# Six buffers for v, six PSUM banks for the first tile's scores, and three loads moved to ACT's queue

## The chip, the cores and the metric

The kernel runs on one core of one Trainium2 chip. The metric is the time on the device in microseconds (us); lower is better. All of the work is done in one launch.

## The reference

Attention with two small matrices that mix the heads, before and after the softmax, followed by two feed-forward layers. B = 4 batches, H = 12 heads, S = 448 positions, D = 64; the layers have 1792 tokens, a model width of 768 and inner widths of 1536 and 2048.

```python
scores = scale * np.matmul(q, k.transpose(0, 1, 3, 2))
scores = np.einsum('bhij,hg->bgij', scores, w_pre)
attn = np.exp(scores - np.max(scores, axis=-1, keepdims=True))
attn = attn / (np.sum(attn, axis=-1, keepdims=True) + 1e-09)
attn = np.einsum('bhij,hg->bgij', attn, w_post)
x = np.matmul(attn, v)                      # then laid out as (1792, 768)
x = (1 / (1 + np.exp(-(x @ w_gate))) * (x @ w_val)) @ w_out
h = np.maximum(x @ w_in, 0.0)
out = (h * h) @ w_out2
```

## The kernel before

The program is written in an order by hand: each engine, and each queue of transfers, runs its instructions in the order in which the Python code emits them, and waits only where an operand or a buffer isn't ready. The engines are TensorE (PE), VectorE (DVE), ScalarE (ACT), GpSimd (POOL) and SyncE (SP). SP issues nearly all transfers, in one queue; ACT can issue some from its own.

**Attention** (`attention`, first some 490 us). Each batch's 448 rows are cut into four row tiles of 120, 120, 100 and 108 rows (`tiles`), and each tile into groups of 10 rows (`groups`), 180 in all. Two tiles make a chunk (`chunks`), eight in all. The main loop (L384) goes over steps s, one group each:

- `scores(n, p)` (L188): for tile n and the pair p of heads, two matmuls (L201; four instructions in the trace) into two PSUM banks of the pool `ps_q`, which has two; ACT copies one bank out (L213), DVE the other (L211), into an `e` buffer (three buffers; in tile 0 the pairs from 3 on use the free buffers of another pool); then transfers `g<-e` (L223) spread the rows over partitions. In tile 0 the rows are in two blocks: the first block's transfers go out at once, some from ACT's queue, the second block's are kept in `second` and go out after all six pairs (L382).
- `premix(s)` (L229): the first mixing matrix `wp` times the spread scores (L237), for two groups, into banks of the pool `ps_m`, which has four.
- `maximum`, `exponent`, `normal` (L245 to L271): the softmax, and the second mixing matrix scaled by the rows' sums (`wn`, on POOL at L266; in the last 14 groups on ACT at L270).
- `postmix(s)` (L275): the second mixing (L282), copied by DVE into `ap` (L294).
- `values(c, h)` (L304): for a chunk c and two heads, 16 matmuls of `ap` and the v tile `vraw` (L311), copied by ACT to `xo` (L326) and stored to `xs` (L327).

Before the loop, the queries and keys of the first tile are loaded in three parts (L373), `masks()` (L127) clears buffers on POOL, loads `w_pre` and `w_post` into `wr` by three small transfers on SP's queue (L133, L137) and makes masks; then come the six `scores(0, p)`, the next tile's queries, and `mixers()` (L155), which makes `wp` and `wq` out of masks and `wr` on DVE.

**The v tiles.** `v_load` (L299) loads one tile of two heads; a chunk uses six of them. The pool `a_v` has four buffers. The first four loads are emitted at steps 4 to 7. After `values` for heads h and h + 1, a buffer is free: if the chunk has another tile to come beyond the four, its load is emitted right then (with the next `flush`), otherwise the buffer is counted in `freed[1]` and filled at one of the next odd steps:

```python
if f is values and (x[1] + 2) % HV == 0:
    if x[1] + 2 + 4 * HV <= H:
        pending.append((load_next, v_load, v_order))
    else:
        freed[1] += 1
```

**The feed-forward layers** (`mlp`) come after. Their work is put in by a planner, `Feed`: tasks have costs, due times (`need`) and buffers out of stocks, and `feed.step` emits those that fit beside the attention's steps; all matmuls of this part are emitted by `feed.finish()` after the attention. Beside the attention it already converts weights (`raw`, `y`, `gv` in the rows) and, from the time on when the last scores are emitted, loads the first inputs `t<-xs` and splits each into two parts (L885: ACT L888, then DVE L891). A split's output takes a buffer of the stock `slots`: five exist from the start (L716), eleven more once the last `postmix` is emitted (`after_mixes`, L723).

Of the kernel before, what the change touches and what calls it, by code (L numbers as in the profile page):

```python
# [9 lines left out]
F32 = mybir.dt.float32  # L10
# [9 lines left out]
P = 128  # L20
JP = 112
GI = 10
HV = 2
# [4 lines left out]
HP = P // 2  # L28
MW, PW, VW, SW, STEP = 0.40, 0.85, 1.66, 0.92, 2.2
KB = 10  # L30
UT = 6


# [34 lines left out]
def attention(tc, feed, q, k, v, w_pre, w_post, xs, B, H, S, D):  # L68
# [10 lines left out]
    nc = tc.nc  # L79
# [22 lines left out]
    with ExitStack() as ctx, ExitStack() as mid, ExitStack() as left:  # L102
        kw = dict(side="right")
        one = ctx.enter_context(tc.tile_pool(name="a_one", bufs=1, **kw))
        pv4 = ctx.enter_context(tc.tile_pool(name="a_v", bufs=4, **kw))
        po = ctx.enter_context(tc.tile_pool(name="a_o", bufs=4, **kw))
        pp = ctx.enter_context(tc.tile_pool(name="a_p", bufs=1, **kw))
        pa = mid.enter_context(tc.tile_pool(name="a_a", bufs=NA, **kw))
# [2 lines left out]
        ps_q = mid.enter_context(tc.tile_pool(name="ps_q", bufs=2, space=PSUM, side="left"))  # L111
# [15 lines left out]
        def masks():  # L127
            nc.gpsimd.memset(wr, 0.0)
            nc.gpsimd.memset(mask, 0.0)
            nc.gpsimd.memset(wp, 0.0)  # L130
            for g in g_of:
                nc.gpsimd.memset(g[:G0], 0.0)
            nc.sync.dma_start(  # L133
                out=wr[G0 : G0 + GI * H, 0, :], in_=w_pre.unsqueeze(0).to_broadcast([GI, H, H])
            )
            for u in range(2):
                nc.sync.dma_start(  # L137
                    out=wr[u * HP : u * HP + KH, 1, :],
                    in_=w_post.unsqueeze(0).to_broadcast([HB, H, H]),
                )  # L140
            for u, m in ((0, first), (0, mask[:HP, :HB]), (1, mask[HP:, HB:])):
                nc.gpsimd.memset(m, 1.0)
                lead = G0 if m is first else 0
                for base, mult in ((-lead, 1), (H - 1 + lead, -1)):
                    nc.gpsimd.affine_select(
                        out=m,
                        in_=m,
                        compare_op=ALU.is_ge,
                        fill=0.0,
                        base=base,  # L150
                        pattern=[[-mult * H, HB], [0, H]],
                        channel_multiplier=mult,
                    )
# [34 lines left out]
        def scores(n, p):  # L188
# [3 lines left out]
            if p == 0:  # L192
                g_t[n] = g_of[n % 2]
            kt = k_t.pop((b, p)) if i0 + rows == S else k_t[b, p]
            ps = [
                ps_q.tile([P, S], F32, tag="q", name="ps_s")
                for _ in range(2)
            ]
            for o in range(2):
                r = slice(o * D, (o + 1) * D)  # L200
                nc.tensor.matmul(  # L201
# [176 lines left out]
        for p in range(NP):  # L378
            scores(0, p)
# [4 lines left out]
        for s in range(NG + 30):  # L384
# [2 lines left out]
            flush()  # L387
            if s < NG:
                maximum(s)
            if s in (4, 5, 6, 7):  # L390
                load_next(v_load, v_order)
            if s >= 8 and s % 4 == 0 and freed[0]:
                load_next(k_load, k_order)
# [14 lines left out]
            while bpos < len(back) and (left_over > 0.5 or s >= NG or late or back[bpos][0] is values and not made):  # L408
# [15 lines left out]
                f(*x)  # L424
                made = made or f is values
                if f is values and (x[1] + 2) % HV == 0:
                    if x[1] + 2 + 4 * HV <= H:
                        pending.append((load_next, v_load, v_order))
                    else:
                        freed[1] += 1  # L430
# [262 lines left out]
def mlp(ctx, tc, xs, wg, wv, wo, wi2, wo2, out):  # L693
# [6 lines left out]
    feed = Feed(tc)  # L700
# [9 lines left out]
    def pool(name, bufs, **kw):  # L710
        return ctx.enter_context(tc.tile_pool(name=name, bufs=bufs, reuse_waits="tile", **kw))
# [1 line left out]
    raws, ys, w32s, ws, slots, brief, xts, cs, gs, banks = (Stock() for _ in range(10))  # L713
    feed.stock(raws, pool("m_r", 2, side="left"), 2)
    feed.stock(ys, pool("m_y", 2, side="left"), 2)
    feed.stock(slots, pool("m_s0", 5, side="left"), 5)  # L716
    dram = pool("m_dram", 1, space=DRAM)

    def after_scores():
# [4 lines left out]
    def after_mixes():  # L724
        feed.stock(w32s, pool("m_w31", 1, side="left"), 1)
        feed.stock(ws, pool("m_w1", 1, side="left"), 1)
        feed.stock(slots, pool("m_s1", 11, side="left"), 11)
        feed.stock(banks, pool("m_ps0", 6, space=PSUM, side="left"), 6)

    def after_all():  # L730
# [473 lines left out]
```

## Time and profile before

| | |
|---|---|
| median of three timed runs | 1369.6 us (1364.2 to 1371.24) |
| the profiled execution | 1377.83 us |
| its span, first to last instruction | 1376.1 us |
| PE busy | 1322.3 us, 96% of the span |
| PE weight load busy | 1067.6 us, 78% |
| DVE busy | 1086.5 us, 79% |
| ACT busy | 764.7 us, 56% |
| POOL busy | 329.3 us, 24% |

All times below are us from the start of the span. A row of the timeline gives the start and the length of one instruction or of several alike in a row (x4 is four), and in brackets how long the engine had been idle just before, and what ended that. "SPq" and "ACTq" are the queues of SP and ACT: their rows are the issuing of transfers, not the transfers themselves. The "granted clock" is TensorE's clock as a share of 2.4 GHz. The DMA share is the mean busy share of the core's 16 transfer engines.

### The profile page before, as it was taken

What the parts mean: (1) busy time and instruction counts of PE and PEld (TensorE: products, weight loads), DVE (VectorE), ACT (ScalarE), POOL (GpSimd) and SP (SyncE); (2) the same over time, 40 slices, a digit from 0 to 9 for tenths busy, and PEclk for the clock granted to TensorE, in tenths of its full rate; (3) what the DMA queues carried; (4) which work ended last, traced back from release to release, by engine and by line L of the source; (5) the groups of instructions that cost most, each with busy time, mean ns of one, the idle gap of its engine ahead of it and who ended that gap; (6) DMA issues with size and microseconds to landing.
All of it is one profiled execution on the core that took longest, in us unless ns stands there. A gap on an engine that the chain in (4) does not pass through costs nothing.

```text
span 1376.1 us, 22485 instructions
## 1 busy us (share of the span) xinstructions
PE 1322.3 (96%) x7604; PEld 1067.6 (78%) x7604; DVE 1086.5 (79%) x1953; ACT 764.7 (56%) x1434; POOL 329.3 (24%) x353
## 2 busy tenths in 40 slices
PE   6879999999999899999999999999999999999998
PEld 2445555564655689999999999999988999999998
DVE  2767786786878878789998788999998986566864
ACT  2544544454455665667666666676655565434553
POOL 3243343343344204340022433003430000000000
PEclk9999999999999999999999999999999999999999
DMA  4768758877676747987478888549885455333343
GB/s 153 232 175 233 235 187 238 235 231 228 206 235 202 266 135 252 318 274 232 119 255 298 309 296 276 164 137 323 281 288 155 119 159 171 104 105 105 112 124 106
DMA packets 146478, 284.61 MB, mean 207 GB/s; under 512 B 17276, under 2 KB 91708, under 8 KB 146364
## 3 DMA queue, kind: packets, MB, share of 16 engines
q1 hardware_dynamic: 145984, 282.61, 65.2%
q8 instruction: 60, 0.98, 0.3%
q10 hardware_dynamic: 380, 0.57, 0.1%
q14 instruction: 54, 0.44, 0.1%
HBM read 180.25 MB, written 63.31 MB: 177 GB/s over the span
## 4 chain that ended last, share of the span: by engine, by line
PE 87%; DVE 5%; DMA 5%; ACT 1%; issue 1%; POOL 0%; SPq 0%; ACTq 0%; DVEq 0%; POOLq 0%
PE ps L903 63%; PE ps_p L282 8%; PE ps_s L201 6%; PE ps_v L311 5%; PE ps_m L237 5%; DMA g<-e 2%; DMA vraw<-in_v 2%; DVE ap L294 2%; DVE nm L248 1%; DVE e L211 1%; DVE y L782 1%; DMA k<-in_k 0%; DVE y L779 0%; ACT e L213 0%; DMA gv<-y 0%
## 5 line engine op out<-in xcount | busy, mean ns | idle before, releaser
L903 PE MATMUL ps<-s,w 128*128 128x448 f32 x4284 | 876.9, 367 | 3.8 <-DVE w L891 3.8
L903 PEld LDWEIGHTS ps<-s,w 128*128 128x128 f32 x4284 | 805.6, 188 | 74.8 <-DVE w L891 4.1
L891 DVE TENSOR_TENSOR w<-w,w 128x768 fp32r<-128x768 f32 x238 | 248.5, 1046 | 95.4 <-ACT w L888 93.8
L888 ACT CAST w<-w 128x768 fp32r<-128x768 f32 x238 | 199.0, 836 | 167.4 <-PE ps L903 147.0
L793 POOL TENSOR_TENSOR y<-y,raw 128x384 int32<-128x384 int32 x136 | 166.9, 1245 | 425.3 <-DVE y L782 127.2
L282 PEld LDWEIGHTS ps_p<-wn,a 128*112 128x112 f32 x1440 | 156.8, 176 | 94.1 <-POOL wn L266 40.2
L282 PE MATMUL ps_p<-wn,a 128*112 128x120 f32 x1440 | 182.0, 274 | 18.7 <-DVE ap L294 8.3
L266 POOL TENSOR_SCALAR wn<-wq,sm 128x120 f32<-128x120 f32 x166 | 113.2, 682 | 274.3 <-DVE sm L263 214.7
L248 DVE TENSOR_REDUCE nm<-ps_m 128x1 f32<-128x448 f32 x180 | 111.0, 617 | 60.0 <-PE ps_m L237 59.9
L255 ACT ACTIVATE a<-ps_m,nm 128x448 f32<-128x448 f32 x180 | 114.4, 636 | 60.3 <-DVE sm L260 52.0
L888 ACT CAST s<-g 128x448 fp32r<-128x448 f32 x196 | 109.9, 566 | 40.5 <-PE ps L903 35.2
L891 DVE TENSOR_TENSOR s<-g,s 128x448 fp32r<-128x448 f32 x196 | 122.0, 633 | 4.6 <-ACT s L888 0.6
L294 DVE COPY ap<-ps_p 112x480 f32<-112x480 f32 x180 | 114.1, 648 | 10.2 <-PE ps_p L282 8.3
L213 ACT COPY e<-ps_s 120x448 f32<-120x448 f32 (+1 forms) x96 | 51.1, 532 | 120.4 <-PE ps_s L201 93.7
L201 PE MATMUL ps_s<-k,q 64*120 64x448 f32 (+1 forms) x384 | 105.1, 615 | 13.1 <-ACT e L213 7.7
L211 DVE COPY e<-ps_s 120x448 f32<-120x448 f32 (+1 forms) x96 | 60.0, 625 | 47.0 <-PE ps_s L201 30.3
L311 PE MATMUL ps_v<-ap,vraw 112*64 112x240 f32 (+1 forms) x768 | 85.7, 369 | 10.8 <-DMA vraw<-in_v 9.4
L237 PE MATMUL ps_m<-g,wp 64*64 64x448 f32 x720 | 92.2, 572 | 3.9 <-DMA g<-e 3.8
L311 PEld LDWEIGHTS ps_v<-ap,vraw 112*64 112x64 f32 x768 | 54.5, 140 | 52.7 <-ACT xo L326 14.4
L201 PEld LDWEIGHTS ps_s<-k,q 64*120 64x120 f32 (+1 forms) x384 | 29.8, 182 | 58.3 <-ACT a L255 17.6
L928 DVE TENSOR_TENSOR c<-ps,c 128x448 f32<-128x448 f32 x104 | 63.9, 619 | 10.1 <-PE ps L903 9.4
L773 ACT ACTIVATE raw<-raw 128x768 f32<-128x768 f32 x68 | 62.0, 912 | 11.9 <-DMA raw<-in_wo 5.2
(44 smaller groups left out, 830.5 us busy)
## 6 DMA issues: line engine op xcount, KB each, us to landing
w<-wo SPq DMA_DIRECT2D x98, 384.0 KB
w<-gv SPq DMA_DIRECT2D x84, 384.0 KB
g<-e SPq DMA_DIRECT2D x132, 210.0 KB
raw<-in_wo SPq DMA_DIRECT2D x56, 384.0 KB
w<-wi SPq DMA_DIRECT2D x56, 384.0 KB
wo<-y SPq DMA_DIRECT2D x42, 384.0 KB
gv<-y SPq DMA_DIRECT2D x36, 384.0 KB
raw<-in_wi SPq DMA_DIRECT2D x32, 384.0 KB
```

What stands on the lines that cost most here:

```text
L201: nc.tensor.matmul(ps[o][:isz], lhsT=q_t[n][r, p, :isz], rhs=kt[r], start=True, stop=True)
L237: nc.tensor.matmul(ps[u * HP : (u + 1) * HP], lhsT=wp[r], rhs=g_t[n][r, 2 * t + u], start=True, stop=True,)
L248: nc.vector.tensor_reduce(out=nm, in_=ps, op=ALU.max, axis=AX.X, negate=True)
L255: nc.scalar.activation(a, ps, AF.Exp, bias=nm, accum_out=sm)
L266: nc.gpsimd.tensor_scalar(out=wn, in0=wq, scalar1=sm, scalar2=None, op0=ALU.mult)
L282: nc.tensor.matmul(ps[:JP, jt], lhsT=a[:, jt * JP : (jt + 1) * JP], rhs=wn.rearrange("p g i -> p (g i)"), start=True, stop=True,)
L294: nc.vector.tensor_copy(ap[c][:, :, :, g0 - i0 : g0 - i0 + rows], ps[:JP, :, :, :rows])
L311: nc.tensor.matmul(ps[o * D : (o + 1) * D, :w], lhsT=vraw[c, (h + o) // HV][:, (h + o) % HV, jt, :], rhs=ap[c][:, jt, h + o, :w], start=jt ...
L793: e.tensor_tensor(out=y3, in0=y3, in1=word(0)[:, i].bitcast(I32), op=ALU.add)
L888: e.copy(dst.tile[:, 0], src.tile)
L891: e.tensor_tensor(out=dst.tile[:, 1], in0=src.tile, in1=dst.tile[:, 0].bitcast(F32), op=ALU.subtract)
L903: e.matmul(bank.tile, lhsT=a[k], rhs=x[l], start=start and n == 0, stop=stop and n == 2, skip_group_check=not fresh,)
```

## The change

- The pool `a_v` gets six buffers (`VB`). The first six v loads are emitted at steps 4 to 9, and each buffer that comes free is then filled at one of the next odd steps (the condition `x[1] + 2 + 6 * 2 <= 12` never holds).
- In tile 0 the pairs 1, 2, 4 and 5 take their two banks from `ps_m`, the pairs 0 and 3 from `ps_q`.
- The three loads of `w_pre` and `w_post` are issued from ACT's queue.
- Of the sixteen `slots`, three in place of five exist from the start, and thirteen in place of eleven come with `after_mixes`.

```diff
+VB = 6
-        pv4 = ctx.enter_context(tc.tile_pool(name="a_v", bufs=4, **kw))
+        pv4 = ctx.enter_context(tc.tile_pool(name="a_v", bufs=VB, **kw))
...
-            nc.sync.dma_start(
+            nc.scalar.dma_start(
                 out=wr[G0 : G0 + GI * H, 0, :], in_=w_pre.unsqueeze(0).to_broadcast([GI, H, H])
             )
             for u in range(2):
-                nc.sync.dma_start(
+                nc.scalar.dma_start(
                     out=wr[u * HP : u * HP + KH, 1, :],
...
-            ps = [
-                ps_q.tile([P, S], F32, tag="q", name="ps_s")
-                for _ in range(2)
-            ]
+            at, tag = (ps_m, "m") if n == 0 and p % 3 else (ps_q, "q")
+            ps = [at.tile([P, S], F32, tag=tag, name="ps_s") for _ in range(2)]
...
-            if s in (4, 5, 6, 7):
+            if 4 <= s < 4 + VB:
                 load_next(v_load, v_order)
...
-                    if x[1] + 2 + 4 * HV <= H:
+                    if x[1] + 2 + VB * HV <= H:
...
-    feed.stock(slots, pool("m_s0", 5, side="left"), 5)
+    feed.stock(slots, pool("m_s0", 3, side="left"), 3)
...
-        feed.stock(slots, pool("m_s1", 11, side="left"), 11)
+        feed.stock(slots, pool("m_s1", 13, side="left"), 13)
```

## Rows read from the trace of the kernel before

**Rows 1.** Busy time by stage: PE, PEld, DVE, ACT, POOL; clock, DMA share.

```profile
0.00:490.00 490.00, 443.43 (x3310) 260.60 (x3312) 360.22 (x909) 233.97 (x575) 182.28 (x242) 0.99 0.71 216
490.00:1376.00 886.00, 878.88 (x4298) 807.03 (x4292) 726.26 (x1044) 530.78 (x859) 147.04 (x111) 1.00 0.63 202
```

**Rows 2.** Timeline of the head: start, length, engine, line, output<-input, count, [idle].

```profile
4.02 1.85 PE L201 MATMUL ps_s<-k,q 64*120 64x448 f32 x4 [4.02 <-DMA k<-in_k]
...
5.10 1.00 SPq L133 DMA_DIRECT2D wr<-in_w_pre  x1
5.87 0.53 ACT L213 COPY e<-ps_s 120x448 f32<-120x448 f32 x1 [3.80 <-PE ps_s L201]
5.91 0.62 DVE L211 COPY e<-ps_s 120x448 f32<-120x448 f32 x1 [5.91 <-PE ps_s L201]
6.15 1.54 SPq L137 DMA_DIRECT2D wr<-in_w_post  x2
...
6.59 1.85 PE L201 MATMUL ps_s<-k,q 64*120 64x448 f32 x4 [0.72 <-DVE e L211]
7.81 12.07 SPq L223 DMA_DIRECT2D g<-e  x8
...
11.89 0.59 POOL L145 TENSOR_SCALAR_AFFINE_SELECT mask<-mask 64x60 f32<-64x60 f32 x2
...
16.69 2.08 PE L201 MATMUL ps_s<-k,q 64*120 64x448 f32 x4 [0.48 <-ACT e L213]
16.90 0.78 ACTq L223 DMA_DIRECT2D g<-e  x1
18.57 0.53 ACT L213 COPY e<-ps_s 120x448 f32<-120x448 f32 x1 [1.93 <-PE ps_s L201]
...
20.46 9.45 SPq L383 DMA_DIRECT2D g<-e  x10
22.59 1.77 PE L237 MATMUL ps_m<-g,wp 64*64 64x448 f32 x8 [3.82 <-DMA g<-e]
```

**Rows 3.** Waits: engine, line <- releaser: us in total, times, longest.

```profile
PE ps_v L311 <- DMA vraw<-in_v: 9.4, 3, 4.9
```

**Rows 4.** Timeline of PE, first chunk's values.

```profile
97.94 1.84 PE L311 MATMUL ps_v<-ap,vraw 112*64 112x240 f32 x16
104.66 3.45 PE L311 MATMUL ps_v<-ap,vraw 112*64 112x240 f32 x16 [4.87 <-DMA vraw<-in_v]
108.04 0.98 PE L237 MATMUL ps_m<-g,wp 64*64 64x448 f32 x8
```

**Rows 5.** Busy time in slices of 2 us, same stretch.

```profile
101.00:103.00 2.00, 0.00 (x0) 0.00 (x0) 0.08 (x1) 0.00 (x0) 0.53 (x1) 1.00 1.00 345
...
105.00:107.00 2.00, 2.00 (x12) 1.35 (x10) 0.00 (x0) 0.00 (x0) 0.00 (x0) 0.50 0.80 267
```

**Rows 6.** Timeline of PE, third and fifth chunk's values.

```profile
220.25 3.18 PE L311 MATMUL ps_v<-ap,vraw 112*64 112x240 f32 x16 [2.31 <-DMA vraw<-in_v]
...
335.81 2.69 PE L311 MATMUL ps_v<-ap,vraw 112*64 112x240 f32 x16 [2.19 <-DMA vraw<-in_v]
338.44 1.76 PE L237 MATMUL ps_m<-g,wp 64*64 64x448 f32 x8
```

**Rows 7.** Busy time, 20 us in the seventh chunk's values.

```profile
430.00:450.00 20.00, 18.91 (x151) 9.86 (x152) 12.31 (x33) 10.19 (x27) 6.28 (x10) 1.00 0.77 240
```

**Rows 8.** Chain of work that ended last: start, us, what.

```profile
83.46 10.06 DMA g<-e
...
97.33 7.19 DMA vraw<-in_v
```

**Rows 9.** Timeline of SP's queue around steps 8 and 9.

```profile
45.20 2.06 SPq L769 DMA_DIRECT2D raw<-in_wg  x3
51.65 1.68 SPq L223 DMA_DIRECT2D g<-e  x2
```

**Rows 10.** Timeline of PE at the end of the mixing steps.

```profile
473.44 1.07 PE L282 MATMUL ps_p<-wn,a 128*112 128x120 f32 x8 [0.77 <-ACT wn L270]
```

## The prediction

> **What bounds the kernel now.** First the stages [rows 1]: in the first 490 us (attention) TensorE (PE) is busy 443.43 us, so it sits idle for 46.6; in the 886 us after them (the two feed-forward layers) it is idle for 7.1. TensorE is the bound in both, and only the first has idle time worth taking. The change touches the first, and the hand-over. Then the timeline of the head [rows 2] and the waits of TensorE in the 490 us. The largest wait for a transfer that repeats is the one of the values step (L311) for `vraw`: 9.4 us in 3 places [rows 3], at 104.66, 220.25 and 335.81 [rows 4, 6].
>
> The profiled execution took 1377.83 us with a span of 1376.1, so 1.7 us lie around the span; the median of the three timed runs is 1369.6. The sum is a saving, worked out within the span, and taken off the median. Within 0.5% (6.85 us) a measurement of this kernel could hardly tell from no change.
>
> **First tile's scores, six banks.** Six pairs of heads each run L201, and each needs two PSUM banks that ACT (0.53) and DVE (0.62) copy out [rows 2]. With two banks, pair p+1 can't start before both copies of pair p are done: TensorE takes 1.85, then idles 0.72 or a little less. From the first pair at 4.02 to the sixth at 16.69 that is 12.67 for five, 2.53 each. With six banks pair p+1 runs while pair p is copied, and a bank comes back two pairs later. Banks of the mixing step are borrowed; its first use of them is at 22.59, after all copies.
> Two prices. At 1.85 a pair, five periods save 5 x (2.53 - 1.85) = 3.4 us. But 1.85 is a low clock: the same eight instructions of the mixing step take 1.77 at 22.59 and 0.98 at 108.04 [rows 2, 4]. After the stall that ends at 104.66 TensorE worked without a break at a granted clock of 0.50 (1.2 GHz), and by 108.04 had 2.4 GHz again [rows 4, 5]. (In the head the column of the granted clock reads 1.00 although the durations are doubled; there I go by the durations.) In the head before, TensorE breaks off after each pair and its sixth pair still takes 2.08; after, it runs unbroken from 4.02, so I expect the faster level for the last three pairs or so, at 1.85 x 0.98/1.77 = 1.02 each. ACT is next late then: on pairs 3 to 5 it copies (0.53) and issues a `g<-e` transfer (0.78) [rows 2], 1.31 per pair. Pairs 0 and 1 end at 5.87 and 7.72, pair 2 about 9.3, pair 3 about 10.3; then copy, issue, copy, issue, copy on ACT bring the sixth copy's end to 10.3 + 0.53 x 3 + 0.78 x 2, about 13.5, where it now is 18.57 + 0.53 = 19.10 [rows 2]: 5.6 us saved.
> What follows is tied to the sixth copy: SP's ten second-block transfers, 9.45 us without a pause, directly behind the next q load, and the mixing step at 22.59 that waits for `g<-e` [rows 2]. Both move with it. The masks on POOL end at 11.89 + 0.59, in time. I take 5.0, nearer to the faster level; ends 3.4 and 6.0.
>
> **Mixing weights on ACT's queue.** SP loses three issues, 1.00 + 1.54 = 2.54 us [rows 2], and its first `g<-e` could go out at the end of the first copy, 6.40, in place of 7.81. SP isn't what ends the head (it waits for the copies), so I add nothing. ACT gains three issues; it is idle for 3.80 before its first copy at 5.87 [rows 2], which holds 2.54 or, at a slower first issue, some 3.3. What waits behind them is that copy, then TensorE. Without this cover the cost is 2.54. The loads also run beside the first q and k loads now, not behind them; nearest row: the k load on which the first scores wait (4.02 of idle, [rows 2]). Bounds: 0.5 gained to 1 lost; I take 0, since by their shapes the three loads move some 11 KB and one k load 224.
>
> **Six buffers for v.** Each chunk of rows uses six v tiles, of two heads each. With four buffers the fifth and sixth can be loaded only when the first and second have been used, and this in a stretch in which the transfer engines are full (share 1.00 at 101 to 103, [rows 5]). In the first chunk the fifth tile's load is issued at 97.33 and takes 7.19 [rows 8]; TensorE, done with the fourth at 97.94 + 1.84 = 99.78, waits for it until 104.66 [rows 4]. With six buffers all six of a chunk are loaded while the chunk before is finished, one per two steps, tens of us ahead. So all three waits should go: 4.87 + 2.31 + 2.19 = 9.37 us [rows 4, 6].
> Each also brings a low clock behind it: sixteen matmuls take 3.45, 3.18 and 2.69 in place of 1.84, and the mixing step at 338.44 takes 1.76 in place of 0.98 [rows 4 to 6]: 1.61 + 1.34 + 0.85 + 0.78 = 4.58. Together 13.95 us at most. A chunk of the same size that met no such wait shows that the other engines can keep pace: 18.91 of 20 us busy at 430 to 450 [rows 7].
> Not all of it stays. In these stretches the `g<-e` transfers are slow as well; one is in the chain for 10.06 us [rows 8], and scores, whose output buffers (three) wait for them, are next late. I take two thirds, 9.5; ends 4.7 (a third) and 14.0.
> The Trainium skill (DMA: Bandwidth & Descriptors, Issuing engines are not separate DMA queues) has a rule that speaks against more: transfers of all queues share the same 16 engines, and another queue saves only the time of issuing. By that, a v tile that lands earlier takes its time from another transfer, and the result would be that of the second rival below, 1362.6 and not 1355.1. The trace agrees that the engines are full at the first stall (1.00, [rows 5]); it shows a share of 0.77 at the chunk without a wait [rows 7], so that there is room elsewhere.
> The two loads that are added at the start, at steps 8 and 9, cost SP 2 x 0.5 us; SP has nothing from 47.26 to 51.65 [rows 9], so nothing is added (1 us if that cover is gone). Later ones move by a step or two; the same number is issued, behind the same stores.
>
> **Three early slots for five.** Two of five split inputs of the feed-forward layer (ACT about 0.55 and DVE about 0.6 each) can no longer be made before the last mixing step. There TensorE waits for ACT (0.77 at 473.44, [rows 10]): a gain of up to 0.8 per split, 1.6. They are made during the last values, when ACT is lightly used; if not, 2 x 0.55 is lost at the hand-over. I take 0; ends 1.6 gained, 1.1 lost.
>
> **Sum**: 5.0 + 0 + 9.5 + 0 = 14.5 us, of the profiled 1377.8 to about 1363.3, and of the median to **1355.1**. All ends at their best: 6.0 + 0.5 + 14.0 + 1.6 = 22, 1347.5. All at their worst: 3.4 - 1 + 4.7 - 1 - 1.1 = 5, 1364.6.
>
> **Rivals.** *All of it* stays: nothing else is late, 5.6 + 13.95, about 1350. For: the undisturbed chunk [rows 7]. Against: [rows 8].
> *The transfers are the next wait.* The v stalls go, but the scores' `g<-e` transfers, which used the pause to land, are late in their place: 4 from the head and 3 from the stalls, 7 us, 1362.6 (1359 to 1367). For: share 1.00 and landings of 7.19 and 10.06 us [rows 5, 8]. Against: SP is held by `vraw` less, and bytes don't grow.
> *The change doesn't do what it says* in the head: the low clock stays, and ACT's three new issues hold the first copy up by their 2.54, so 3.4 - 2.5 = 0.9; of the stalls a fifth comes back, 2.8: 3.7 in all, 1365.9. Against it is the unbroken work after 104.66 that did bring the clock up [rows 4, 5].
> *Slower*: the extra v traffic at each chunk makes `g<-e` late in all tiles. From the point on where such a transfer lands later than the three buffers last, scores stop in every tile. Priced like the second stall's idle time, 2.31 [rows 6], in the 14 tiles after the head: 32 us lost against 14.5 gained, 1387. For: one landing of 10.06 did hold up ACT [rows 8]. Against: this needs it in every tile, and bytes are unchanged.
>
> **How the numbers follow.** Forecast 0.52 (1350 to 1360 by itself), all of it 0.12, transfers next 0.24, head fails 0.06, slower 0.06. Faster by over 0.5% means under 1362.8: 0.52 + 0.12 + half of 0.24 = 0.76. Within: 0.12 + 0.06 = 0.18. Slower 0.06. The range of 8 in 10 leaves out the slower case, the failed head, and the outer parts of the first two rivals (some 0.03 and 0.05): 1347 to 1365.
>
> **What would show it.** Right: six L201 calls at the start without the 0.7 us pauses, the last ones near 1 us; the first L237 at about 17 and not 22.59; no L311 row with `vraw` as its releaser; the last values at about 475 and not 490. Wrong: L237 at 19 or later (the clock or ACT); new waits of the scores for `g<-e` at 90 to 105; a TensorE pause between the last values and the first L903. The forecast fails most likely at the size of the v term.

## The result, and the profile after

In twenty timed runs of each kernel the changed kernel took 1359.55 us (median, 1352.29 to 1373.32) and the kernel before 1372.41 (1364.2 to 1389.07): a ratio of 0.9894, with a 95% interval of 0.9871 to 0.9916. On the 1369.6 us from which the prediction started, that is a saving of 14.5 us (11.5 to 17.7). The two medians by themselves are 12.9 us apart; the ratio, which leaves out runs over 1.5% above the fastest of their kernel, is what the text goes by. A second comparison of the same two kernels (below) gave 0.9923, a saving of 10.5 us (5.2 to 15.9). Predicted were 14.5 and a time of 1355.1, in a range of 1347 to 1365. The sum came out as forecast, to the tenth by luck; the terms behind it did not all do so, and that is what the rest is about.

The profiled execution took 1360.46 us with a span of 1358.7; before it was 1377.83 and 1376.1. Busy time by stage in the kernel after, with the columns of [rows 1] (the last values step ended at 490.36 before and ends at 479.65 now; the same first stretch is shown so that the lines can be compared):

```profile
0.00:490.00 490.00, 449.15 (x3362) 269.39 (x3363) 367.95 (x922) 240.66 (x590) 180.50 (x242) 0.98 0.73 219
490.00:1358.00 868.00, 862.91 (x4243) 796.16 (x4241) 723.15 (x1032) 520.80 (x845) 150.43 (x111) 1.00 0.63 204
```

Of the 17.4 us between the two spans, 10.7 lie in attention (490.36 - 479.65) and 6.7 behind it, where the prediction expected nothing. The waits of TensorE in the first 490 us of the kernel after (line <- releaser: us in total, times, longest):

```profile
PE ps_p L281 <- DVE ap L293: 9.3, 14, 2.8
PE ps_m L236 <- DMA q<-in_q: 7.1, 1, 7.1
PE ps_p L281 <- POOL wn L265: 6.3, 7, 1.8
PE ps_s L200 <- ACT e L212: 5.6, 7, 2.0
...
PE ps_m L236 <- DMA gv<-y: 2.2, 1, 2.2
```

The row of [rows 3], 9.4 us of the values step waiting for `vraw`, is gone: no transfer is a releaser of L310 (L311 before) any more. New are the wait of 7.1 of the first mixing step, 3.8 before, and one of 2.2 for a transfer in the stretch where the first `vraw` wait had been.

**The head after** (start, length, engine, line, operation, count, [idle <- releaser]), to be read against [rows 2]:

```profile
0.94 1.41 ACTq L134 DMA_DIRECT2D wr<-in_w_pre  x1
...
2.38 1.55 ACTq L138 DMA_DIRECT2D wr<-in_w_post  x2
...
3.96 1.28 ACT L212 ACT_TABLE_LOAD   x1 [3.96 <-issue]
3.97 7.24 PE L200 MATMUL ps_s<-k,q 64*120 64x448 f32 x24 [3.97 <-DMA k<-in_k]
4.73 0.33 SPq L184 DMA_DIRECT2D q<-in_q  x1
5.10 2.38 SPq L176 DMA_DIRECT2D k<-in_k  x2
5.82 0.53 ACT L212 COPY e<-ps_s 120x448 f32<-120x448 f32 x1 [0.58 <-PE ps_s L200]
...
7.59 7.28 SPq L222 DMA_DIRECT2D g<-e  x8
...
12.19 0.53 ACT L212 COPY e<-ps_s 120x448 f32<-120x448 f32 x1 [0.37 <-DVE wp L160]
...
18.33 1.77 PE L236 MATMUL ps_m<-g,wp 64*64 64x448 f32 x8 [7.12 <-DMA q<-in_q]
...
24.46 1.74 PE L236 MATMUL ps_m<-g,wp 64*64 64x448 f32 x8
```

All six pairs of scores are now one unbroken row of 24 matmuls, 7.24 us long. The sixth copy on ACT ends at 12.19 + 0.53 = 12.72, 6.4 earlier than the 19.10 before. The mixing step comes only 4.26 earlier (22.59 to 18.33): TensorE waits 7.12 us for it. SP has issued the first block's eight `g<-e` by 7.59 + 7.28 = 14.87, and 3.5 us later the step starts. The row names the next tile's q load, which this step doesn't read and which was issued directly behind the eight; that the step waits for the `g<-e` to land is concluded from what it reads, and from the same row in eight of the ten profiles with six banks, the change's second one among them, which names `g<-e`.

**The first chunk's values after**, against [rows 4]:

```profile
95.70 3.46 PE L310 MATMUL ps_v<-ap,vraw 112*64 112x240 f32 x32
...
100.00 1.84 PE L310 MATMUL ps_v<-ap,vraw 112*64 112x240 f32 x16
...
105.96 0.61 PE L236 MATMUL ps_m<-g,wp 64*64 64x448 f32 x4 [2.17 <-DMA gv<-y]
```

The fifth tile's matmuls stand directly behind the fourth's (32 in one row), at the full clock, where before there were 4.87 us of idle and 3.45 us at half of it. But just behind them TensorE stops again, for 2.17 us.

### The profile page after: what moved, and what is told of

Same layout as the page of the kernel before. It is cut to its first block, busy times and chain, and to the rows that moved or that the text cites. A ratio compares the mean times of both kernels' runs of the same rounds, so it can differ in the third digit from the quotient of the medians.

```text
span 1358.7 us, 22455 instructions
## 1 busy us (share of the span) xinstructions
PE 1312.1 (97%) x7604; PEld 1065.5 (78%) x7604; DVE 1091.1 (80%) x1953; ACT 761.5 (56%) x1434; POOL 330.9 (24%) x353
## 4 chain that ended last, share of the span: by engine, by line
PE 88%; DVE 5%; DMA 5%; issue 1%; ACT 1%; POOL 0%; SPq 0%; DVEq 0%; ACTq 0%; POOLq 0%
PE ps L902 64%; PE ps_p L281 9%; PE ps_s L200 5%; PE ps_v L310 5%; PE ps_m L236 5%; DMA g<-e 3%; DVE ap L293 2%; DVE nm L247 1%; DVE y L781 1%; DVE e L210 1%; DMA xs<-xo 1%; DMA k<-in_k 1%; POOL wn L265 0%; DVE y L778 0%; DMA gv<-y 0%
## 5 line engine op out<-in xcount | busy, mean ns | idle before, releaser
L902 PE MATMUL ps<-s,w 128*128 128x448 f32 x4284 | 871.6, 366 | 2.4 <-DVE w L890 2.4
L902 PEld LDWEIGHTS ps<-s,w 128*128 128x128 f32 x4284 | 804.2, 188 | 69.6 <-DVE w L890 3.5
L792 POOL TENSOR_TENSOR y<-y,raw 128x384 int32<-128x384 int32 x136 | 170.3, 1270 | 428.8 <-DVE y L781 138.3
L887 ACT CAST s<-g 128x448 fp32r<-128x448 f32 x196 | 109.7, 565 | 42.3 <-PE ps L902 36.9
L310 PEld LDWEIGHTS ps_v<-ap,vraw 112*64 112x64 f32 x768 | 52.5, 136 | 41.1 <-ACT xo L325 14.4
L310 PE MATMUL ps_v<-ap,vraw 112*64 112x240 f32 (+1 forms) x768 | 81.3, 358 | 1.5 <-DVE ap L293 1.2
L927 DVE TENSOR_TENSOR g<-g 128x448 f32<-128x448 f32 x112 | 71.0, 664 | 0.6
```

Of the source, the lines that this page charges most:

```text
L310: nc.tensor.matmul(ps[o * D : (o + 1) * D, :w], lhsT=vraw[c, (h + o) // HV][:, (h + o) % HV, jt, :], rhs=ap[c][:, jt, h + o, :w], start=jt ...
L792: e.tensor_tensor(out=y3, in0=y3, in1=word(0)[:, i].bitcast(I32), op=ALU.add)
L887: e.copy(dst.tile[:, 0], src.tile)
L902: e.matmul(bank.tile, lhsT=a[k], rhs=x[l], start=start and n == 0, stop=stop and n == 2, skip_group_check=not fresh,)
L927: e.tensor_tensor(out=out.tile, in0=a.tile, in1=b.tile, op=op)
```

## The experiments

Each experiment answers one question; all were run beside the kernel before. "The start of the values" is the first chunk's first values step (88.73 before, 86.91 after), and "the end of attention" is where the last values step ends (490.36 before, 479.65 after). Both are from the profiled execution of each.

### Which part brings the time

**The six banks alone.**

```diff
-            ps = [
-                ps_q.tile([P, S], F32, tag="q", name="ps_s")
-                for _ in range(2)
-            ]
+            at, tag = (ps_m, "m") if n == 0 and p % 3 else (ps_q, "q")
+            ps = [at.tile([P, S], F32, tag=tag, name="ps_s") for _ in range(2)]
```

> The kernel before with the six banks for the first tile's scores alone. Theory: the head's gain is in place at the first mixing step (22.59 before, 18.33 after the whole change; here 18 to 18.7), but about half of it is lost again by the first values (88.73 before; here 86 to 87.5), and the last values end 2 to 4 us before 490.4. Rival: the whole gain of 4.3 is carried to the end of the last values (486). Second rival: it is gone by the end, because the next stretches wait for transfers and not for TensorE (490). Of the whole time 0.998 to 0.9965 of before.

Measured: 0.9989 (0.9955 to 1.0023), or 1.5 us saved with an interval from 3.2 lost to 6.2 gained. The timeline of its head and of its first chunk's values:

```profile
3.98 7.18 PE L199 MATMUL ps_s<-k,q 64*120 64x448 f32 x24 [3.98 <-DMA k<-in_k]
...
18.65 1.77 PE L235 MATMUL ps_m<-g,wp 64*64 64x448 f32 x8 [7.49 <-DMA q<-in_q]
...
83.19 1.84 PE L309 MATMUL ps_v<-ap,vraw 112*64 112x240 f32 x16
...
96.64 3.47 PE L309 MATMUL ps_v<-ap,vraw 112*64 112x240 f32 x16 [3.53 <-DMA vraw<-in_v]
```

The head is that of the change, so the banks alone make it; the mixing step is 3.94 us earlier, the start of the values even 5.5 (88.73 to 83.19), and attention ends at 485.07, 5.3 earlier. The `vraw` waits stay: four of them, 8.7 us in all, where three took 9.4. So in this one trace the head's gain is carried to the end of attention, as the first rival had it, and the theory's loss before the first values did not come. The time shows less, 1.5 us, but its interval holds 5.3 too, so what the head is worth in the whole isn't settled.

**Six v buffers alone**, with their loads and their order, on the kernel before:

```diff
+VB = 6
...
-        pv4 = ctx.enter_context(tc.tile_pool(name="a_v", bufs=4, **kw))
+        pv4 = ctx.enter_context(tc.tile_pool(name="a_v", bufs=VB, **kw))
...
-            if s in (4, 5, 6, 7):
+            if 4 <= s < 4 + VB:
...
-                    if x[1] + 2 + 4 * HV <= H:
+                    if x[1] + 2 + VB * HV <= H:
```

> The kernel before with the six v buffers alone (slots as before). Theory: the three waits for vraw go, 15 us are gained at them and 6 given back in the stretches after them, so that the last values end 8 to 10 us before 490.4 (480 to 482.5) and the time is 0.994 of before. Rival: without the head's shift nothing is given back, the last values end 13 to 15 us earlier, 0.990. Second rival: transfers take the place of v, 3 us or less.

Measured: 0.994 (0.9899 to 0.9981), 8.2 us saved (2.6 to 13.8). No wait for `vraw` is left, and attention ends at 481.77, 8.6 us earlier, although its values start only at 95.62. One cause of the late start is a new pause before it, in the timeline of TensorE:

```profile
63.72 1.15 PE L202 MATMUL ps_s<-k,q 64*100 64x448 f32 x4 [2.37 <-ACT e L214]
```

**The weight loads alone.**

```diff
-            nc.sync.dma_start(
+            nc.scalar.dma_start(
                 out=wr[G0 : G0 + GI * H, 0, :], in_=w_pre.unsqueeze(0).to_broadcast([GI, H, H])
             )
...
-                nc.sync.dma_start(
+                nc.scalar.dma_start(
```

> The kernel before with the mixing weights on ACT's queue alone. Theory: SP's third q and last two k loads are issued later, as after the whole change (4.73 to 7.48 in place of 3.60 to 4.99), and the first g<-e at about 7.6 in place of 7.81: nothing is won, first mixing step at 22.3 to 22.7, the last values end within 0.5 of 490.4. Rival (the prediction's): SP is free by 5.0 and issues its first g<-e at 6.4.

Measured: 1386.22 in one run, attention ending at 492.21. The timeline of its head:

```profile
4.90 0.33 SPq L183 DMA_DIRECT2D q<-in_q  x1
5.27 1.36 SPq L175 DMA_DIRECT2D k<-in_k  x2
...
6.83 13.08 SPq L223 DMA_DIRECT2D g<-e  x8
...
22.60 1.77 PE L237 MATMUL ps_m<-g,wp 64*64 64x448 f32 x8 [3.80 <-DMA g<-e]
```

SP's first `g<-e` goes out about 1 us earlier (7.81 to 6.83), and the mixing step is where it was, 22.60 against 22.59. This part is worth nothing where it was meant to work. The single time of 1386 says little against it: attention ends 1.9 us later than before, less than two profiles of one kernel differ by, and the other 6.5 us lie behind attention, where this trace has the slower of two paces from about 730 on (last section).

**The slots alone.**

```diff
-    feed.stock(slots, pool("m_s0", 5, side="left"), 5)
+    feed.stock(slots, pool("m_s0", 3, side="left"), 3)
...
-        feed.stock(slots, pool("m_s1", 11, side="left"), 11)
+        feed.stock(slots, pool("m_s1", 13, side="left"), 13)
```

> The kernel before with three early slots and thirteen late ones alone. Theory: nothing moves, the last values end within 0.5 of 490.4 and TensorE goes on without a pause. Rival: up to 1.6 gained in the last mixing steps, because two splits no longer stand between them. Second rival: a pause of 1 us or more at the start of the feed-forward layers.

Measured: 1369.4 in one run; attention ends at 488.53, 1.8 earlier than before, again less than two profiles of one kernel differ by. TensorE's instructions keep their order, but from about 475 us on, 598 of DVE's 1953 instructions and 369 of ACT's 1434 stand at another place in their engine's order: the planner lays out the feed-forward work anew. There the trace does differ. Between the two feed-forward layers TensorE waits for DVE, which makes a weight tile `w`. In the kernel before:

```profile
1032.76 3.57 PE L903 MATMUL ps<-s,w 128*128 128x448 f32 x9 [3.77 <-DVE w L891]
```

Busy time in the 20 us from the start of that pause (PE, PEld, DVE, ACT, POOL; clock, share of the transfer engines), kernel before:

```profile
1028.99:1048.99 20.00, 16.23 (x71) 14.70 (x72) 17.87 (x24) 9.91 (x17) 4.40 (x4) 0.91 0.61 195
```

The same 20 us of the run with the slots alone:

```profile
1029.98:1049.98 20.00, 17.63 (x88) 16.35 (x88) 19.25 (x27) 12.48 (x21) 8.22 (x6) 1.00 0.70 242
```

And of the change, first the pause and then the stretch:

```profile
1023.47 2.70 PE L902 MATMUL ps<-s,w 128*128 128x448 f32 x12 [2.36 <-DVE w L890]
...
1021.11:1041.11 20.00, 17.64 (x87) 16.37 (x88) 19.27 (x27) 12.44 (x21) 8.23 (x6) 1.00 0.71 243
```

The pause is 3.77 before and 2.37 with the slots alone, and the granted clock keeps at 1.00, where it is 0.91 on average behind the longer pause. 88 matmuls in place of 71 fit into the same 20 us.

**The change without the slots** was to test that from the other side.

```diff
-    feed.stock(slots, pool("m_s0", 3, side="left"), 3)
+    feed.stock(slots, pool("m_s0", 5, side="left"), 5)
...
-        feed.stock(slots, pool("m_s1", 13, side="left"), 13)
+        feed.stock(slots, pool("m_s1", 11, side="left"), 11)
```

> The changed kernel, but with the slots as before (five early, eleven late). Theory: the slots part is worth 4 to 5 us, not in the attention but in the feed-forward layers, because the planner's order on DVE is another one from there on: here TensorE's pause for w near 1020 is 3.4 to 4.5 us long with a low clock after it, as in the kernel before and in the runs with the banks and with v alone, and not 2.4; and the matmuls behind it come at 244 per 50 us and not 248. Ratio 0.9925 to 0.994. Rival: the slots do nothing, the pause and the pace differ from run to run by chance: ratio 0.9894 as of the whole change.

Measured: 0.9878 (0.98 to 0.9956). The interval runs from 12.9 us below the change's own 0.9894 to 8.5 above it, so the time tells nothing about the slots. The pause does: 3.49. Over all kernels run, those with 5 and 11 slots have pauses of 3.77 (before), 4.45, 3.76, 3.40 and 3.49, those with 3 and 13 have nine from 2.22 to 2.38. Within 20 us from its start the first five run 71, 68, 65, 68 and 73 matmuls, 69 on average, the nine others 78 to 88, 82 on average. At the 0.2024 us of a matmul further on (300 us hold 1482 of them) these 13 are worth 2.6 us. That gain repeats in every trace; no time resolved it.

### Why the head's gain shrinks on its way

In the trace of the change 4.26 us are won at the first mixing step, and 1.8 at the start of the values. In between it has a pause that the kernel with the banks alone does not have. Timeline of ACT and TensorE in the kernel after:

```profile
56.16 0.53 ACT L212 COPY e<-ps_s 100x448 f32<-100x448 f32 x1 [4.17 <-DMA g<-e]
...
56.75 1.93 PE L200 MATMUL ps_s<-k,q 64*100 64x448 f32 x4 [1.99 <-ACT e L212]
```

ACT could not copy the scores out, since the buffers of `e` are freed by `g<-e` transfers and none had landed; TensorE stopped for 2.0 us, and then ran at a granted clock of 0.50 (1.2 GHz):

```profile
58.00:60.00 2.00, 2.00 (x10) 0.30 (x8) 0.16 (x1) 0.00 (x0) 0.58 (x1) 0.50 0.64 230
```

The suspect was the two v loads that the change adds at steps 8 and 9, just ahead of it.

**The same two loads, later.**

```diff
-            if 4 <= s < 4 + VB:
+            if s in (4, 5, 6, 7, 15, 19):
```

> The changed kernel, but with the fifth and sixth v load at steps 15 and 19 in place of 8 and 9. Theory: these two loads fill the transfer engines at 38 to 52 us, the g<-e transfers of the third tile land late, and the scores wait (pause of 2.0 at 54.75, and a low clock after it): here the pause goes and the first values start at 83 to 84.5 in place of 86.9, the last values end 2 to 3 us before 479.65. Rival: the pause comes from the head's shift against the weights' loads, not from v: first values at 86.5 to 87.5.

**Five buffers of `e` in place of three**, loads as in the change.

```diff
-        p4 = left.enter_context(tc.tile_pool(name="a_4", bufs=3, side="left"))
+        p4 = left.enter_context(tc.tile_pool(name="a_4", bufs=5, side="left"))
```

> The changed kernel with five buffers for the scores' copies (e) in place of three. Theory: the scores stop because a g<-e transfer of 8 to 10 us holds its buffer longer than three pairs take; with five the pauses at 54.75 and 85.04 go, first values at 83 to 85, the last values end 3 to 6 us before 479.65. Rival: the transfers are late whatever waits for them, and the pause moves to the mixing step that reads g: first values at 86 to 87.5, the end within 1 of 479.65.

Measured: with the late loads 1364.77 and with five buffers 1365.05, one run each. Both run through where the change stops at 55; the late loads keep a shorter stop of 0.74 at 58, the five buffers none. TensorE at that place with the late loads:

```profile
54.53 1.00 PE L200 MATMUL ps_s<-k,q 64*100 64x448 f32 x4
```

The transfer engines' share in the 18 us before the pause tells the two cures apart (last columns: granted clock, share, GB/s). With the banks alone, whose head is as early but which has no early loads:

```profile
36.00:54.00 18.00, 16.47 (x124) 9.80 (x120) 14.27 (x39) 7.43 (x21) 5.27 (x9) 1.00 0.83 250
```

Kernel after:

```profile
36.00:54.00 18.00, 16.45 (x122) 9.78 (x122) 13.94 (x39) 7.10 (x19) 5.24 (x9) 1.00 0.96 243
```

With the late loads:

```profile
36.00:54.00 18.00, 16.46 (x122) 9.79 (x121) 14.24 (x39) 7.58 (x21) 5.24 (x9) 1.00 0.86 249
```

The early loads bring it from 0.83 to 0.96, the late ones to 0.86. The rate does not rise with it (250, 243 and 249 GB/s): in this stretch the engines are busy longer for no more bytes, and why stays open. With five `e` buffers the share stays at 0.95, and the scores outlast the late landing. Five profiles have both the early loads and three buffers of `e`, and in these the scores wait for ACT's `e` between 54 and 64 us for 2.0 us in all (the change), 1.8 (the change again), 1.7 (without the slots), 3.1 (with eight `xo`, below) and 2.4 (v buffers alone). In the nine others it is 0.74 at most. That the two early loads cause it is shown. At the next stage it seems to cost some 2 us: the values start at 84.89 and 84.71 in these two runs, and at 86.91 in the change. Over all profiles with six banks and six v buffers, the five with a cure start them at 84.19 to 86.87 (85.4 on average), the four without at 86.91 to 88.90 (87.7), so the groups touch, and one run of each could not tell them apart. Whether the 2 us reach the end isn't shown (below).

### What the pause at 104 is, and whether the change can be bettered

**Eight output buffers** were to test a theory on the second pause, at 103.79: that SP, which issued a finished tile's last `g<-e` at 99.23, though it was copied at about 94.2, was held up by stores of values that waited for one of the four `xo` buffers.

```diff
-        po = ctx.enter_context(tc.tile_pool(name="a_o", bufs=4, **kw))
+        po = ctx.enter_context(tc.tile_pool(name="a_o", bufs=8, **kw))
```

> The changed kernel with eight buffers for the values' copies (xo) in place of four. Theory: without the v stall the six values of the first chunk follow each other so closely that ACT waits for an xo buffer whose store hasn't landed (3.05 at 101.62), the exponents behind it are late, and the next mixing step pauses TensorE for 2.17 at 103.79: here that pause goes, the second chunk's values start at 142 to 143 in place of 144.5. Rival: the mixing step waits for its g<-e transfer or for the engines' time, and the pause stays.

Measured: 1358.76 in one run, no pause at 104, and the second chunk's values at 142.69. For one run the theory stood; but the change's own second profile, with four buffers and a pause of 1.75 there, has these values at 142.47. **All three cures together** (late loads, five `e`, eight `xo`) were to beat the change:

> The changed kernel with five e buffers, eight xo buffers and the fifth and sixth v load at steps 15 and 19, all three together. Theory: the three waits that took back part of the v term's and the head's gain were waits for transfers that hold buffers; with more buffers the last values end at 466 to 470 (479.65 after the change, 470.54 with the e buffers alone), TensorE's pauses in the attention sum to 30 us or less (40.4 after the change), and the time is 0.979 to 0.984 of before. Rival: the e buffers had already taken all that there was, 470 to 471.5 and 0.983 to 0.986.

Measured: 0.9913 (0.9879 to 0.9947). It is not better than the change's 0.9894. There is no pause at 55 and the values start at 84.19, but attention ends at 477.16 and not at 466 to 470, TensorE's pauses in it sum to 36.9 us and not to 30, and the pause at 104 is back, although it has eight `xo` buffers:

```profile
102.71 0.98 PE L236 MATMUL ps_m<-g,wp 64*64 64x448 f32 x8 [2.35 <-DMA gv<-y]
```

So the theory on the `xo` buffers falls. The row names `gv`, which this step doesn't read; the matching row of the change without the slots names what it does read:

```profile
106.59 0.98 PE L236 MATMUL ps_m<-g,wp 64*64 64x448 f32 x8 [2.95 <-DMA g<-e]
```

It is the first mixing step of a new tile, and it waits for a `g<-e` transfer. What makes that late stays open: `xo` buffers, `e` buffers and early v loads are each excluded as the only cause. The kernel with five `e` buffers had no such pause in its first profile and one of 2.79 in its second, so it comes and goes in one and the same program.

**The head's issues on two queues**, on top of these three. One more of the first block's `g<-e` and four more of the second's go out from ACT:

```diff
-                        queue = nc.scalar if n == 0 and o and p in (1, 3, 4, 5) else nc.sync
+                        queue = nc.scalar if n == 0 and o and p in (0, 1, 3, 4, 5) else nc.sync
...
-            (nc.scalar if m in (3, 7) else nc.sync).dma_start(out=x, in_=y)
+            (nc.scalar if m % 2 else nc.sync).dma_start(out=x, in_=y)
```

> The same, and one more first-block transfer and four more second-block transfers of the first tile are issued by ACT in place of SP. Theory: the head's first mixing step (18.33) waits for SP, which issues eight transfers in 7.3 us without a pause; with seven it comes at 17.2 to 17.8, SP's second block ends near 20.5 in place of 23.8, and the first values start 1 to 2 us earlier than in the run with all buffers. Rival: the landing of the transfers sets the mixing step, not their issue, 18.0 to 18.6, and the first values don't move.

Measured: 0.9936 (0.9905 to 0.9968). The timeline of its head:

```profile
7.16 6.82 SPq L222 DMA_DIRECT2D g<-e  x7
...
18.48 1.77 PE L236 MATMUL ps_m<-g,wp 64*64 64x448 f32 x8 [6.97 <-DMA g<-e]
```

SP is done with the first block 0.9 us earlier than in the change, at 13.98, and the mixing step is at 18.48 and not before 18.33. The landing of these transfers sets it, not their issue. What it is in the landing wasn't tried. The first values do not move forward either: they start at 86.87, 2.7 us later than in the run with all three cures.

**The change once more, and five `e` buffers timed**, so that the one-run differences get a yardstick:

> The changed kernel once more, unchanged. Theory: the attention repeats (last values end within 1.5 of 479.65, pause for w near 1020 2.2 to 2.5 us), while the pace of the matmuls of the feed-forward layers, 248 or 244 per 50 us, is set anew by chance at each pause and differs from the first profile somewhere; ratio within 0.985 to 0.994. Rival: the pace repeats as well, 244 up to about 620 and 248 from there on, and belongs to the program.

> The changed kernel with five e buffers once more, now timed. Theory: its earlier attention (last values end at 470.54, against 479.65 and 476.06 in two profiles of the changed kernel) repeats, within 1.5; ratio 0.981 to 0.986. Rival: the run with all buffers (477.16) shows what five e buffers are worth, and 470.54 was chance: last values at 475 to 478, ratio 0.988 to 0.993 as of the change itself.

Measured: the change again 0.9923 (0.9884 to 0.9962), five `e` buffers 0.9884 (0.9841 to 0.9927). The intervals overlap by about half of each. The same kernel with five `e` buffers, whose attention ended at 470.54 in its first profile, ended it at 481.46 in the second, so that this first value was chance. The change ended it at 479.65 and at 476.06, not within the 1.5 us of the theory. An end of attention repeats to some 5 us either way, and no variant stands out of that: all nine profiles with six v buffers and six banks lie between 470.5 and 481.5, 477.5 on average; the three profiles without either (before, the weight loads alone, the slots alone) lie between 488.5 and 492.2. The means of the two groups (490.4 and 477.5) are 12.8 apart, which is what the change gains in attention, and the groups don't overlap. No version was found that is shown to beat the change.

## Why the prediction was right, point by point

**The sum** of 14.5 us was met (11.5 to 17.7), but no measurement here is fine enough to make the agreement to a tenth more than luck: the second comparison of the same kernels gave 10.5 (5.2 to 15.9). Run alone, the two terms that carry the sum came out smaller than forecast, 1.5 and 8.2, though both forecasts lie inside the intervals, and one term that was put at nothing is some 2.6 in the traces.

**Six banks: 5.0 predicted.** Up to the copies the working held and was even cautious. The busy time of the kernel after in slices of 2 us:

```profile
4.00:6.00 2.00, 2.00 (x6) 1.17 (x8) 0.13 (x1) 1.42 (x2) 2.00 (x2) 1.00 0.96 269
6.00:8.00 2.00, 2.00 (x8) 0.84 (x6) 1.11 (x2) 0.89 (x2) 2.00 (x1) 1.00 0.73 204
8.00:10.00 2.00, 2.00 (x12) 0.94 (x9) 0.85 (x2) 0.81 (x2) 2.00 (x1) 1.00 0.65 184
```

Matmuls per 2 us go from 6 to 8 to 12 in unbroken work (the clock's column reads 1.00 all along, as it did before), so the last pairs do run at about half the time of the first, and the sixth copy ends 6.4 us earlier, against 5.6 predicted. The step that failed is "Both move with it": the mixing step does not follow the sixth copy. Once the copies were early, the landing of the transfers was late in their place, and 4.26 were left. That was a term mis-sized by 0.7. The faster level does not outlast the wait either:

```profile
18.00:20.00 2.00, 1.67 (x8) 0.33 (x8) 0.00 (x0) 0.00 (x0) 0.00 (x0) 0.50 0.63 230
```

Behind the 7.12 us of idle the granted clock is 0.50, and the second mixing step, at 24.46, still takes 1.74. In the kernel before it took 0.98:

```profile
27.89 0.98 PE L237 MATMUL ps_m<-g,wp 64*64 64x448 f32 x8
```

There 3.4 of the 4.26 are left. The larger loss came behind it: at the start of the values 1.8 and 1.0 were left in the two profiles of the change (86.91 and 87.77 against 88.73). With the banks alone 5.5 were there at the same place and 5.3 at the end of attention, and 1.5 (3.2 lost to 6.2 gained) in the time. So whether the head is worth its 5.0 in the whole stays open; in the change most of it is gone by the first values, in part by the early loads.

**Weight loads: 0 predicted, 0 found** at the mixing step (22.60 against 22.59). The cover named, 3.80 us of idle ACT, held, with little to spare: the three issues end at 3.93, ACT's table load of 1.28, which stood at 0.79 before, comes behind them at 3.96, and 0.58 of idle is left before the first copy, which starts at 5.82 and before at 5.87. But SP's gain was less than put down: 7.81 to 7.59 in the change, not to 6.40, because SP's own k and q issues came later (last section). The Trainium skill (DMA: Bandwidth & Descriptors, Issuing engines are not separate DMA queues) says that issuing on another engine saves only the issuing time; the trace of the weight loads alone agrees, with about 1 us saved at the issue and none at the mixing step.

**Six v buffers: 9.5 predicted, 8.2 measured alone (2.6 to 13.8).** In the change all three waits of [rows 3] are gone, as is the low clock behind them, and the values of the three chunks of [rows 4, 6] became shorter by 7.1, 4.2 and 4.0 us (first chunk: 88.73 to 110.79 before, 86.91 to 101.84 after), 15.3 where 13.95 was put as the most. Between the chunks 6.5 was given back, 4.1 of it between the end of the first and the start of the second (110.79 to 149.39 before, 38.60; 101.84 to 144.52 after, 42.68): 8.9 net from the first values to the end of attention. These 4.1 are the 2.17 at 104 and a second wait, at the first mixing step of the next tile:

```profile
135.53 0.98 PE L236 MATMUL ps_m<-g,wp 64*64 64x448 f32 x8 [1.76 <-ACT a L254]
```

(ACT's instruction named there had ended 0.7 us earlier, so what the step waited for isn't known.) In the second profile of the change this wait isn't there, 2.7 in all was given back, and 13.3 is left. The two thirds that the prediction took were a choice between the ends, and that one profile came close to them and the other to the whole is luck; the mechanism for the missing third, `g<-e` that land late, was named, and the new wait at 104 is one. The one at 55 was not foreseen. "SP has nothing from 47.26 to 51.65, so nothing is added" priced the two early loads by the queue that issues them. SP had the room; the first two of the scores' transfers behind the loads are issued no later than with the banks alone, whose row is the second:

```profile
45.76 2.07 SPq L222 DMA_DIRECT2D g<-e  x2
...
46.45 1.68 SPq L221 DMA_DIRECT2D g<-e  x2
```

But the share of the transfer engines in 36 to 54 went from 0.83 to 0.96, and the scores' transfers that ran beside the loads landed late. That is the step that failed, by some 2 us at 55.

**Slots: 0 predicted, about 2.6 found**, in another place than where it was looked for. The working looked at the hand-over (the L282 step that waits for ACT, [rows 10]), where indeed nothing moved: these waits are 2.6 us in four places before and after. But a planner's stock changes its whole order afterwards, and the gain stands at 1020 to 1030, in the pause for `w`. It is worked out from counts of matmuls in the traces, and no timed comparison confirmed it.

**The rivals.** *The transfers are the next wait* was right in its places (scores waiting at 55, mixing at 18 and 104, all for `g<-e`) and too low in the 7 us that it left of the gain: attention alone gained 10.7 and 14.3 in the two profiles of the change, and the saving measured was 14.5 (11.5 to 17.7), in the second comparison 10.5 (5.2 to 15.9), which by itself would not exclude 7. The rule of the Trainium skill (DMA: Bandwidth & Descriptors, Issuing engines are not separate DMA queues) that led to the same 1362.6 fits the late scores at 55, but the transfers that lost their place cost less than was gained. *All of it stays* failed on these same pauses. *The change doesn't do what it says in the head* failed: the clock did rise. *Slower* failed: the new waits for `g<-e` that the trace shows for sure behind the head are in two places, 55 and 104, and not one per tile.

**The signs named.** The last pairs near half the time, no `vraw` releaser and an end of attention near 475 (479.65 and 476.06) came as described; the first mixing step is at 18.33, between the 17 called right and the 19 called wrong; new waits of the scores for `g<-e` at 90 to 105 had been called wrong, and one such wait is there, at 104, of the mixing step and not of the scores. TensorE has no pause between the last values and the first L902. The forecast was met with the one sign against it by offsetting: the wait took 2.2 us, and the slots' 2.6, which were not forecast, are about as much.

## What to carry to other kernels

A load that is moved earlier is to be priced by the share of the transfer engines at its new place, and not only by the room on its queue: at a share of 0.83 two more loads of one tile each made other transfers late, though the queue had room. When a head is shortened, ask at each step what releases the next one (here copies, then landings), and count a gain only where the last stage still shows it: of 6.4 us at the copies 4.3 arrived at the mixing step and 1 to 1.8 at the values. Before an experiment of one run is read, profile the same kernel twice: here the end of attention differed by 11 us between two profiles of one kernel (470.54 and 481.46).

## What the runs showed of the hardware

**Two paces of the same matmuls at the same granted clock.** In the feed-forward layers TensorE runs without a break, and yet stretches of the same program hold different numbers of matmuls. Kernel after:

```profile
500.00:600.00 100.00, 100.00 (x486) 90.81 (x485) 84.05 (x107) 58.54 (x89) 38.40 (x29) 1.00 0.81 274
...
1040.00:1340.00 300.00, 300.00 (x1482) 278.00 (x1481) 229.25 (x353) 166.00 (x280) 0.00 (x0) 1.00 0.46 133
```

The very same program, run once more:

```profile
500.00:600.00 100.00, 100.00 (x495) 92.68 (x494) 87.17 (x108) 60.90 (x91) 41.29 (x32) 1.00 0.84 288
...
600.00:1020.00 420.00, 419.85 (x2031) 380.78 (x2030) 369.57 (x518) 266.68 (x429) 98.37 (x73) 1.00 0.72 236
```

And the kernel before, which was at the faster pace in 500 to 1020, in the last stretch:

```profile
1040.00:1340.00 300.00, 300.00 (x1453) 272.51 (x1452) 222.55 (x340) 162.71 (x275) 0.00 (x0) 1.00 0.45 129
```

In 300 us there are 1482 matmuls or 1453, one per 202.4 ns or 206.5, 2% apart; the granted clock reads 1.00 in both. Of the fourteen profiles, all with the same 7604 matmuls in them, five have 1482 in this stretch, eight 1453 or 1454, and one, whose pause for `w` reaches into it, 1439. The pace changes near 600, 720 and 1020 to 1040, where TensorE pauses or is slower for some microseconds, one way in one run and the other way in the next. Over up to 850 us it is worth up to some 16 us (2% of 850 is 17). In the nine profiles with six banks and six v buffers the stretch behind attention takes from 879.1 us to 892.8. That helps to explain why the times of one kernel spread from 1352 to 1373, and makes single times such as 1386.22 and 1358.76 say little. Of the 6.7 us that the two profiles differ by behind attention, some 4 are an estimate from it: the kernel before is at the slower pace for 342 us, from 1034 on, the change for 128, up to 608, and 2% of the difference is 4; the other 2.6 are the shorter pause for `w`. What sets the pace stays open. All five profiles with 5 and 11 slots have the slower pace after 1040, and four of the nine with 3 and 13. If the slots favoured the faster one, that would be worth up to 29 matmuls or 5.9 us beside the 2.6 above; but nine slower ones among fourteen fall so by chance in 1 of 16 cases, and it wasn't tested.

**Issues on ACT's queue came with later ones on SP's.** When ACT issued the three small weight loads at the start (0.94 to 3.93), SP's own issues behind its second pair of k loads came later. Each is no longer than before (0.33 to 0.43 us), but there are pauses between them: the third q load went from 3.60 to 4.73 (4.90 with this part alone), and the last two k loads, 0.91 from the start of one to the end of the other before, took 2.38 in the change and 1.36 with this part alone. In all ten profiles with the weight loads on ACT the third q load is issued at 4.58 to 5.14, in the four others at 3.60 or 3.61. Of the 2.54 us taken off SP's queue, 0.1 to 1.0 came out as an earlier first `g<-e`. Why SP pauses, at the end even after ACT's issues are over, stays open.
